# Eight decodings of a weight matrix moved to fixed units of the first batch and tied to the source's order

## The chip, the core and the metric

The kernel runs on one core of one Trainium2 chip. What counts is the device time of one execution in microseconds (us), as the median of several runs. The program is one straight line of instructions without loops at run time: TensorE (PE in the profile, its weight loads PEld), VectorE (DVE), ScalarE (ACT), GpSimd (POOL) and the queue that issues the transfers (SP) each take their own list of instructions in order, and wait for one another through semaphores.

## The reference

Causal block attention feeds a spatially gated block, which feeds a residual block of two dense layers. Batch 4, 8 heads, 576 positions, head dimension 64, all in float32:

```python
scores = scale * q @ k.T                      # masked by blocks of 64 positions
attn   = softmax(scores);  x = attn @ v       # heads joined: x is [4, 576, 512]
h      = relu(x @ w_in)                       # w_in [512, 1024]: u and v halves
gated  = u * (w_spatial @ normalize(v) + b_spatial)
x2     = gated @ w_out
out    = x2 + relu(normalize(x2) * g_ln @ w_ch1) @ w_ch2
```

## The kernel before, in words

**Decoding.** The weights arrive in device memory as 64-bit floats, that is, as pairs of 32-bit words. `decode` (line 81) makes a float32 out of such a pair: one ScalarE instruction on the high words (line 88), one VectorE shift on the low words (line 89), and one VectorE instruction that joins the two (line 90). `split` (line 94) then makes of every float32 a high part and a rest, which TensorE multiplies separately. For `w_in` both halves of the split are on GpSimd: a `tensor_scalar` (line 101) and a subtraction (line 102), since `PLAN['dh']` is `'g'`.

**The stage around the change.** `w_in` is decoded in eight pieces of 128x512 by the generator `decode_in` (line 420). Its first step only issues three loads of 512 KB from the SP queue (line 427); three buffers hold raw pieces (`bufs=3`, line 426). Each later step decodes and splits one piece and then issues the load three pieces ahead, so that the load of piece 3 waits until piece 0 has been read. The loop at line 532 runs over the units `u` of the attention: 16 pairs of heads (four batches of four), nine units to a pair. Unit 0 of a pair is the tail of 64 rows of both heads, the other eight are the four blocks of 128 rows of each head, the longest first. Each unit traces, in this order: the scores on TensorE (lines 250 to 281), the masked maximum on VectorE (line 296) and the exponential on ScalarE (line 303), the transposes of the unit two before it (line 353) with their copies out on VectorE (line 345, tails and blocks of index 3) or ScalarE (line 347, blocks of index 0 to 2), at unit 7 and unit 2 of a pair the product with v (line 404), at unit 5 the scaling and splitting of the pair before (`store_x`, lines 411 to 418, all on GpSimd: lines 414, 60 and 417), one step of `prepare` for the next pair (line 198: its `q` and `k` split, on VectorE line 56, ScalarE lines 58, 212 and 225, and GpSimd lines 209 or 221 and 223), and last the decoding, in the first four pairs at the units whose index in their pair leaves 1 when divided by 3 (`PLAN['pace']` is 3). So the loads start in unit 1, and the eight decodings are traced in units 4, 7, 10, 13, 16, 19, 22 and 25. The first products that need `w_in` are traced from unit 44 on (`value_tile`, line 445, matmuls of lines 106 to 108); they need all of `xT`, too, which `store_x` writes.

**The order on the engines.** The source gives each instruction its rank only. A planner in the build simulates the machine with its own estimates of durations and arrivals, and gives each engine (and the SP queue) its list: of what is ready by its estimate, the lowest rank goes first. An instruction can thus stand well before or behind its place in the source. The chip keeps to the list as it is. `tc.keep_in_program_order(ins)` ties one instruction behind the one traced just before it on its engine; what is traced later may still pass it. The other two users of `decode` (lines 640 and 700) give it that function as `here`; `decode_in` doesn't, and `here` is then a function that does nothing.

Of the kernel before, what the change touches and what calls it, by code (L numbers as in the profile page):

```python
# [19 lines left out]

PLAN = {'mm': 3, 'sc': 3, 'tr': 2, 'D': 2, 'hi0': 'v', 'hi1': 's', 'klo0': 'g', 'klo1': 'g', 'qlo0': 'g', 'qlo1': 'g', 'xm0': 'g', 'xm1': 'g', 'xh0': 'g', 'xh1': 'g', 'xl0': 'g', 'xl1': 'g', 'dm': 'g', 'dh': 'g', 'ev0': 3, 'ev1': 2, 'rate': 24500.0, 'vrb': 3, 'ds': 2, 'dy': 1, 'raw': 5, 'yn': 2, 'ts': 3, 'ring': 8, 'wt': 2, 'cb': 1, 'hq': 8, 'packed': 4, 'plain': 3, 'pre': 8, 'py': 10, 'pyn': 4, 'dn0': 2, 'dnn': 5, 'vl': 'v', 'pace': 3, 'wd': 7, 'tl0': 'v', 'tl1': 'v', 'xe': 's', 'pt': 6, 'dstart': 8}


def f32(ap):
    return ap.bitcast(F32)
# [8 lines left out]
def tile_kernel(  # L34
# [26 lines left out]
    NB, NP, _, _, _, S = qk.shape  # L61
# [19 lines left out]
    def decode(raw, m, e, out, here=lambda ins: ins):  # L81

        low, high = raw[:, :, 0], raw[:, :, 1]
        here(nc.scalar.activation(m, f32(high), AF.Prelu, scale=2.0**-112, alpha=2.0**32))  # L88
        here(nc.vector.tensor_scalar(e, low, 29, None, op0=ALU.logical_shift_right))
        nc.vector.scalar_tensor_tensor(  # L90
            out.bitcast(U32), m.bitcast(U32), 3, e, op0=ALU.logical_shift_left, op1=ALU.bitwise_or
        )

    def split(src, hi, lo, high="s", low="g"):

        if high == "s":
            nc.scalar.copy(hi, src)  # L97
        elif high == "v":
            nc.vector.tensor_copy(hi, src)
        else:  # L100
            nc.gpsimd.tensor_scalar(hi, src, 1.0, 0.0, op0=ALU.mult, op1=ALU.add)
        {"v": nc.vector, "g": nc.gpsimd}[low].tensor_tensor(lo, src, f32(hi), op=ALU.subtract)  # L102
# [80 lines left out]
    def warm(n):  # L183
        for _ in range(n):
            tc.keep_in_program_order(MM(idle, lhsT=zeros[:, 0:128], rhs=zeros, start=True, stop=True))
# [101 lines left out]
    def softmax(u):  # L287

        j, c = UNITS[u % NU]
        banks = state[u]  # L290
        sm = sums[u // NU]
        pt = tail if c == 4 else at.tile([128, 512], F32, tag="p", name="p", bufs=PLAN['pt'])
        nm = at.tile([128, 2], F32, tag="nm", name="nm", bufs=4)
        for i, (s_ps, o, n) in enumerate(banks):
            m = mask[:, 0:n] if c == 4 else mask[:, 512 - n:512]
            nc.vector.tensor_tensor_reduce(  # L296
                pt[:, o:o + n], s_ps[:, :n], m, -0.125, 3e38, ALU.add, ALU.min, nm[:, i:i + 1]
            )
        if c == 4:
            nc.vector.tensor_tensor(nm[:, 0:1], nm[:, 0:1], nm[:, 1:2], op=ALU.min)  # L300
        n = o + n
        col = 8 if c == 4 else 4 * j + c
        nc.scalar.activation(  # L303
            pt[:, :n], pt[:, :n], AF.Exp, bias=nm[:, 0:1], scale=-1.0, accum_out=sm[:, col:col + 1]
        )
        state[u] = (pt, n)
# [3 lines left out]
    def reciprocals(p):  # L310

        sm = sums.pop(p)
        nc.vector.tensor_scalar(sm, sm, 1e-9, None, op0=ALU.add)
        nc.vector.reciprocal(sm, sm)
        ps = p_tr.tile([128, 512], F32, tag="tr", name="rps")
        nc.tensor.transpose(ps[:9, :128], sm, idn)
        rr = at.tile([128, 128], F32, tag="rr", name="rr", bufs=1)
        nc.scalar.copy(rr[:9], ps[:9, :128])
        nc.sync.dma_start(out=r_d[p, :, 0:512].rearrange("j (c q) -> j c q", q=128), in_=rr[:8])
        nc.sync.dma_start(out=r_d[p, :, 512:S], in_=rr[8:9])  # L320
        rb = at.tile([128, S], F32, tag="rb", name="rb")
        for j in range(2):
            nc.sync.dma_start(out=rb[64 * j:64 * j + 64], in_=r_d[p, j].partition_broadcast(64))
        rb_t[p] = rb
# [13 lines left out]
    def transposes(u):  # L338
        j, c = UNITS[u % NU]
        pt, n = state.pop(u)  # L340

        def put(src, dst):
            out = dst(pT_of(u // NU)[1 if c >= 2 else 0])
            if c >= PLAN["ev1" if u >= NU * NP else "ev0"] and not (c == 4 and PLAN["tl1" if u >= NU * NP else "tl0"] == "s"):
                nc.vector.tensor_copy(out, src)  # L345
            else:
                nc.scalar.copy(out, src)

        def flip(k0, k1):
            tr = p_tr.tile([128, 512], F32, tag="tr", name="tr")  # L350
            for kc in range(k0, k1):
                o = 128 * (kc - k0)
                nc.tensor.transpose(tr[:, o:o + 128], pt[:, 128 * kc:128 * kc + 128], idn)  # L353
            return tr

        if c == 4:
            tr = flip(0, 4)
            put(
                tr.rearrange("p (r h q) -> p r h q", h=2, q=64),
                lambda t: view(t, 256, [[WH, 4], [5 * WH, 2], [1, 64]]),  # L360
            )
            tr = flip(4, 5)
            put(tr[:, 0:128].rearrange("p (h q) -> p h q", q=64), lambda t: t[:, :, 4 * WH + 256:5 * WH])
        else:
            tr = flip(0, c + 1)
            put(
                tr[:, :n].rearrange("p (r q) -> p r q", q=128),
                lambda t: view(
                    t, (5 * WH if c >= 2 else 2 * WL) * j + 128 * (c % 2), [[WH if c >= 2 else WL, c + 1], [1, 128]]
                ),  # L370
            )
# [5 lines left out]
    def tick():  # L377
        for e in list(slow):
            e[0] -= 1
            if e[0] <= 0:  # L380
                slow.remove(e)
                e[1]()

    def flush():
        todo, later[:] = list(later), []
        for f in todo:
            f()
# [32 lines left out]
    def decode_in():  # L420
        raws = {}

        def fetch(i):
            if i < 2 * KD:
                kc, h = divmod(i, 2)
                raws[i] = dn.tile([128, F, 2], U32, tag="hl", name="raw", bufs=3)
                nc.sync.dma_start(
                    out=raws[i].rearrange("p a b -> p (a b)"), in_=wi32[:, kc, 2 * F * h:2 * F * h + 2 * F]
                )

        fetch(0)
        fetch(1)
        fetch(2)
        yield
        for i in range(2 * KD):
            kc, h = divmod(i, 2)
            m = dn.tile([128, F], F32, tag="vr", name="dm", bufs=PLAN["vrb"])
            e = dn.tile([128, F], U32, tag="ur", name="de")
            cols = slice(F * h, F * h + F)
            decode(raws.pop(i), m, e, m)  # L440
            split(m, win[0][:, kc, cols], win[1][:, kc, cols], PLAN['dh'])
            fetch(i + 3)
            yield
# [57 lines left out]
    dense = None  # L501
    debt = 0.0
    dec = decode_in()
    preps = {}

# [23 lines left out]
    size = [200 + (S if c == 4 else 128 * (c + 1)) for _, c in UNITS]  # L529
    tot = float(sum(size) * NP)  # L530
    D = PLAN['D']
    for u in range(NS + 8):
        p, i = divmod(u, NU)
        if u < NS:
            scores(u)
            if u < 3:
                warm(3)
            softmax(u)
        tick()
        flush()  # L540
        if D <= u < NS + D:
            transposes(u - D)
        if i == PLAN['wd'] and p < NPAIR:
            weighted(p, 1)
        if i == 0 and 1 <= p <= NPAIR:
            reciprocals(p - 1)
        if i == D and 1 <= p <= NPAIR:
            weighted(p - 1, 0)
        if i == D + 3 and 1 <= p <= NPAIR:
            store_x(p - 1)  # L550
        if i == 0:
            for q in range(2, PACKED) if p == 0 else range(max(p + 2, PACKED), p + 3):
                load(q)
            load_v(p + 2)
            if p + 1 < NPAIR:
                preps[0] = prepare(p + 1)
        if 0 in preps and i >= 1:
            next(preps[0], None)
        if p < NP:
            if i % PLAN['pace'] == 1:  # L560
                next(dec, None)
        else:
            b, k = divmod(u, NU * NP)
            if k == PLAN['dstart'] and b <= NB - 1:
                dense = chain(dense, w_in_stage(b - 1))
            fill(PLAN['rate'] * size[i] / tot)
# [81 lines left out]
    dec = decode_out()  # L648
# [24 lines left out]
    raws = {}  # L673
# [441 lines left out]
def _layout(np, q, k, v, moe_w_in, moe_w_spatial, moe_b_spatial, moe_w_out, moe2_g_ln, moe2_w_ch1, moe2_w_ch2):  # L1115

    B, H, S, D = q.shape
    qk = np.stack([q, k], axis=2).reshape(B, H // 2, 2, 2, S, D).transpose(0, 1, 5, 2, 3, 4)
# [40 lines left out]
```

## Time and profile before

| what | value |
|---|---|
| device time, median of 3 runs | 808.03 us (807.02 to 809.18) |
| the profiled execution's own time | 806.9 us |
| its span in the profile | 805.0 us |
| TensorE busy | 783.6 us (97%) |
| VectorE, ScalarE, GpSimd busy | 526.8, 420.3, 414.6 us |

The span runs from the first to the last instruction of the profiled execution; its own time has 1.9 us more around it. Times in rows are microseconds from the start of the span unless a column says ns. An engine's share of the whole span is a mean over stages with different limits; for this change the first 85 us are what to look at. The granted clock (PEclk) is TensorE's, as a share of full speed, with 1.00 for 2.4 GHz and 0.50 for 1.2 GHz.

### The profile page before, as it was taken

What the parts mean: (1) busy time and instruction counts of PE and PEld (TensorE: products, weight loads), DVE (VectorE), ACT (ScalarE), POOL (GpSimd) and SP (SyncE); (2) the same over time, 40 slices, a digit from 0 to 9 for tenths busy, and PEclk for the clock granted to TensorE, in tenths of its full rate; (3) what the DMA queues carried; (4) which work ended last, traced back from release to release, by engine and by line L of the source; (5) the groups of instructions that cost most, each with busy time, mean ns of one, the idle gap of its engine ahead of it and who ended that gap; (6) DMA issues with size and microseconds to landing.
All of it is one profiled execution on the core that took longest, in us unless ns stands there. A gap on an engine that the chain in (4) does not pass through costs nothing.

```text
span 805.0 us, 13277 instructions
## 1 busy us (share of the span) xinstructions
PE 783.6 (97%) x4498; PEld 671.3 (83%) x4498; DVE 526.8 (65%) x1193; ACT 420.3 (52%) x1071; POOL 414.6 (51%) x417
## 2 busy tenths in 40 slices
PE   9899999999999999899999999999999999999997
PEld 4567788778878799899988888888899888888986
DVE  5866666674565277776677787897566588645534
ACT  5688676566755454555363554553344454433421
POOL 5799656654553343232275455455545465545431
PEclk9799999999999999999999999999999999999999
DMA  8927645445241569688520343204001003000002
GB/s 236 257 66 191 177 126 159 127 140 160 67 157 61 151 210 291 208 250 271 173 92 1 97 125 94 79 0 157 1 15 39 1 1 127 18 0 1 1 1 78
DMA packets 53687, 88.66 MB, mean 110 GB/s; under 512 B 6770, under 2 KB 17138, under 8 KB 53620
## 3 DMA queue, kind: packets, MB, share of 16 engines
q1 hardware_dynamic: 53620, 87.83, 36.7%
q8 instruction: 35, 0.57, 0.3%
q14 instruction: 32, 0.26, 0.1%
HBM read 68.85 MB, written 18.95 MB: 109 GB/s over the span
## 4 chain that ended last, share of the span: by engine, by line
PE 76%; DMA 7%; DVE 7%; issue 3%; POOL 3%; SPq 2%; ACT 2%; POOLq 0%; ACTq 0%; DVEq 0%
PE hps L938 21%; PE o L106 8%; PE o L108 8%; PE o L107 8%; PE pv L404 5%; PE tr L353 4%; PE sc L281 3%; DMA raw<-in_w_in_dram 2%; PE ups L106 2%; PE by L106 2%; PE ups L108 2%; PE ups L107 2%; PE by L108 2%; PE by L107 2%; DMA raw<-in_w_ch_dram 1%
## 5 line engine op out<-in xcount | busy, mean ns | idle before, releaser
L102 POOL TENSOR_TENSOR a<-s,a 128x256 fp32r<-128x256 f32 x96 | 78.2, 818 | 93.3 <-ACT a L97 93.3
L107 PE MATMUL o<-w,h 128*128 128x512 f32 x288 | 112.9, 393 | 0.0
L106 PE MATMUL o<-w,h 128*128 128x512 f32 x288 | 107.8, 398 | 1.4 <-ACT h L930 1.4
L944 DVE TENSOR_TENSOR c<-hps,c 128x384 f32<-128x384 f32 x120 | 66.5, 554 | 55.0 <-PE hps L938 53.3
L108 PE MATMUL o<-w,h 128*128 128x512 f32 x288 | 97.6, 397 | 0.2
L296 DVE CUSTOM_DVE_ANT_0 p<-sc,mask 128x512 f32<-128x512 f32 (+3 forms) x128 | 58.6, 478 | 43.2 <-PE sc L281 21.0
L303 ACT ACTIVATE p<-p,nm 128x512 f32<-128x512 f32 (+3 forms) x128 | 71.2, 558 | 28.4 <-DVE nm L296 25.8
L102 POOL TENSOR_TENSOR a<-w,a 128x256 fp32r<-128x256 f32 x72 | 60.7, 845 | 44.7 <-ACT a L97 38.7
L97 ACT CAST a<-s 128x256 fp32r<-128x256 f32 x96 | 38.4, 404 | 83.5 <-PE hps L938 75.3
L345 DVE COPY pH<-tr 128x512 f32<-128x512 f32 (+1 forms) x88 | 49.8, 574 | 24.7 <-PE tr L353 23.9
L106 PEld LDWEIGHTS o<-w,h 128*128 128x128 f32 x288 | 53.7, 188 | 12.0 <-ACT h L930 2.7
L107 PEld LDWEIGHTS o<-w,h 128*128 128x128 f32 x288 | 54.1, 188 | 10.1
L353 PE MATMUL tr<-idn,p 128*128 128x128 f32 x320 | 56.4, 283 | 6.1 <-DVE pH L345 6.1
L108 PEld LDWEIGHTS o<-w,h 128*128 128x128 f32 x288 | 53.2, 188 | 8.8 <-DVE h L931 1.0
L788 POOL TENSOR_TENSOR gt<-gf,gt 128x576 fp32r<-128x576 f32 (+1 forms) x17 | 25.3, 1493 | 60.7 <-ACT gt L787 60.7
L117 POOL TENSOR_TENSOR rs<-rs,nhalf 128x1 f32<-128x1 f32 x36 | 23.5, 654 | 62.6 <-DVE rs L116 62.4
L353 PEld LDWEIGHTS tr<-idn,p 128*128 128x128 f32 x320 | 38.4, 142 | 16.6 <-DVE pH L345 8.5
L88 ACT ACTIVATE dm<-raw 128x256 f32<-128x256 f32 (+1 forms) x72 | 32.1, 464 | 32.4 <-DVE w L90 8.8
L221 POOL TENSOR_TENSOR stack<-qkt,stack 64x576 fp32r<-64x576 f32 x24 | 34.0, 1417 | 26.1 <-ACT stack L58 23.7
L931 DVE SCALAR_TENSOR_TENSOR h<-c,h 128x384 fp32r<-128x384 f32 x72 | 44.7, 642 | 1.5 <-ACT h L930 1.5
L281 PE MATMUL sc<-stack 128*128 128x512 f32 (+3 forms) x192 | 43.8, 342 | 0.8 <-DVE nm L296 0.2
L930 ACT ACTIVATE h<-c 128x384 fp32r<-128x384 f32 x72 | 35.3, 521 | 16.2 <-DVE c L944 15.9
(183 smaller groups left out, 2265.8 us busy)
## 6 DMA issues: line engine op xcount, KB each, us to landing
raw<-in_w_ch_dram SPq DMA_DIRECT2D x64, 256.0 KB
qkt<-in_qk_dram SPq DMA_DIRECT2D x112, 144.0 KB
vt<-in_v_dram SPq DMA_DIRECT2D x16, 320.0 KB
rb<-r_d SPq DMA_DIRECT2D x32, 144.0 KB
u_d<-ur SPq DMA_DIRECT2D x16, 288.0 KB
us<-u_d SPq DMA_DIRECT2D x16, 288.0 KB
y_d<-ys SPq DMA_DIRECT2D x18, 256.0 KB
yr<-y_d SPq DMA_DIRECT2D x18, 256.0 KB
```

The costliest lines, as they stand in the source:

```text
L102: {"v": nc.vector, "g": nc.gpsimd}[low].tensor_tensor(lo, src, f32(hi), op=ALU.subtract)
L106: MM(out_ps, lhsT=a[0], rhs=b[0], start=first, stop=False)
L107: MM(out_ps, lhsT=a[0], rhs=b[1], start=False, stop=False)
L108: MM(out_ps, lhsT=a[1], rhs=b[0], start=False, stop=last)
L281: MM(s_ps[:, :nn], lhsT=st[:, j, i, q], rhs=st[:, j, 2, 0:nn], start=(i == 0), stop=(i == 1))
L296: nc.vector.tensor_tensor_reduce(pt[:, o:o + n], s_ps[:, :n], m, -0.125, 3e38, ALU.add, ALU.min, nm[:, i:i + 1])
L303: nc.scalar.activation(pt[:, :n], pt[:, :n], AF.Exp, bias=nm[:, 0:1], scale=-1.0, accum_out=sm[:, col:col + 1])
L345: nc.vector.tensor_copy(out, src)
L353: nc.tensor.transpose(tr[:, o:o + 128], pt[:, 128 * kc:128 * kc + 128], idn)
L931: nc.vector.scalar_tensor_tensor(t[:, 1], src, 0.0, f32(t[:, 0]), op0=ALU.max, op1=ALU.subtract)
L938: MM(ps, lhsT=a[x], rhs=b[y], start=not more and kc == 0 and k == 0, stop=kc == KD // 2 - 1 and k == 2, skip_group_check=True,)
L944: nc.vector.tensor_tensor(out, ps, x, op=ALU.add)
```

## The change

`decode_in` now passes `tc.keep_in_program_order` to `decode`, so that the ScalarE instruction and the VectorE shift of each piece are tied behind what was traced just before them on their engine. And the decodings no longer follow the rhythm of three: the loads still start in unit 1, and the eight decodings are traced in units 8, 12, 16, 20, 23, 26, 29 and 32.

```diff
@@ decode_in @@
-            decode(raws.pop(i), m, e, m)
+            decode(raws.pop(i), m, e, m, tc.keep_in_program_order)
@@ before the loop over the units @@
+    DECODE = {1, 8, 12, 16, 20, 23, 26, 29, 32}
@@ in the loop, after the step of prepare @@
-        if p < NP:
-            if i % PLAN['pace'] == 1:
-                next(dec, None)
-        else:
+        if u in DECODE:
+            next(dec, None)
+        if p >= NP:
             b, k = divmod(u, NU * NP)
```

## Rows read from the trace of the kernel before

**Rows 1.** The page: span, busy time of each engine.

```profile
span 805.0 us, 13277 instructions
...
PE 783.6 (97%) x4498; PEld 671.3 (83%) x4498; DVE 526.8 (65%) x1193; ACT 420.3 (52%) x1071; POOL 414.6 (51%) x417
```

**Rows 2.** The chain that ended last, 12 to 60 us: start, length, what.

```profile
15.06 8.81 DMA raw<-in_w_in_dram
...
24.47 8.08 DMA raw<-in_w_in_dram
```

**Rows 3.** Stretches between three products with v: length, busy (count) by engine, clock, DMA.

```profile
20.27:38.35 18.08, 14.86 (x79) 9.74 (x78) 14.52 (x35) 11.02 (x33) 14.03 (x14) 0.77 1.04 259
38.35:52.48 14.13, 13.79 (x91) 9.27 (x90) 11.18 (x35) 12.15 (x33) 12.32 (x12) 0.93 0.50 121
52.48:64.37 11.89, 11.54 (x84) 8.42 (x83) 7.97 (x30) 10.29 (x31) 11.31 (x11) 1.00 0.26 77
```

**Rows 4.** The same view in steps of 2 us: PE, PEld, DVE, ACT, POOL, clock.

```profile
24.00:26.00 2.00, 1.47 (x14) 1.13 (x13) 2.00 (x6) 2.00 (x7) 2.00 (x3) 1.00 1.02 274
26.00:28.00 2.00, 1.62 (x9) 1.08 (x9) 2.00 (x3) 0.70 (x4) 2.00 (x2) 0.65 1.09 204
28.00:30.00 2.00, 2.00 (x11) 1.29 (x11) 1.01 (x4) 0.74 (x2) 2.00 (x3) 0.50 1.01 220
30.00:32.00 2.00, 0.91 (x6) 0.47 (x5) 2.00 (x4) 0.88 (x4) 2.00 (x2) 1.00 1.02 248
32.00:34.00 2.00, 0.77 (x5) 0.54 (x6) 1.44 (x6) 0.97 (x2) 1.71 (x2) 0.86 1.02 364
34.00:36.00 2.00, 2.00 (x9) 1.78 (x9) 2.00 (x9) 1.37 (x5) 0.55 (x3) 0.50 1.00 338
36.00:38.00 2.00, 2.00 (x6) 1.09 (x5) 0.94 (x5) 1.05 (x2) 2.00 (x4) 0.50 1.05 245
38.00:40.00 2.00, 2.00 (x8) 0.80 (x9) 2.00 (x4) 1.54 (x4) 1.23 (x1) 0.50 1.04 225
```

**Rows 5.** Waits, 20 to 43 us: engine line <- releaser: us, times, longest.

```profile
ACT dm L88 <- DMA raw<-in_w_in_dram: 4.7, 3, 2.6
...
DVE de L89 <- DMA raw<-in_w_in_dram: 2.4, 3, 1.0
```

**Rows 6.** ScalarE in order of time: start, length, line, out<-in.

```profile
20.20 0.70 ACT L88 ACTIVATE dm<-raw 128x512 f32<-128x512 f32 x1
...
24.78 0.57 ACT L347 COPY pL<-tr 128x256 f32<-128x256 f32 x2
...
40.22 0.78 ACT L303 ACTIVATE tail<-tail,nm 128x576 f32<-128x576 f32 x1
...
42.23 0.66 ACT L88 ACTIVATE dm<-raw 128x512 f32<-128x512 f32 x1
```

**Rows 7.** The decodings' instructions, 0 to 60 us: ns min/median/max, first and last start.

```profile
L89 DVE TENSOR_SCALAR de<-raw x8: 361/528/1055, 19.9 to 40.2; 128x512 uint32<-128x512 uint32 x8
...
L88 ACT ACTIVATE dm<-raw x8: 663/676/700, 20.2 to 42.2; 128x512 f32<-128x512 f32 x8
L90 DVE SCALAR_TENSOR_TENSOR dm<-dm,de x8: 679/817/1293, 21.8 to 44.4; 128x512 uint32<-128x512 uint32 x8
L101 POOL TENSOR_SCALAR win<-dm x8: 618/784/1119, 22.6 to 46.6; 128x512 fp32r<-128x512 f32 x8
L102 POOL TENSOR_TENSOR win<-dm,win x8: 1261/1366/1733, 24.1 to 49.0; 128x512 fp32r<-128x512 f32 x8
```

**Rows 8.** GpSimd in order of time: start, length, line, idle before and releaser.

```profile
22.58 1.59 POOL L101 TENSOR_SCALAR win<-dm 128x512 fp32r<-128x512 f32 x2 [3.55 <-DVE dm L90]
...
65.30 1.41 POOL L223 TENSOR_TENSOR stack<-qkt,stack 64x576 fp32r<-64x576 f32 x1
...
80.48 1.42 POOL L417 TENSOR_TENSOR xT<-xx,xT 128x576 fp32r<-128x576 f32 x1
```

**Rows 9.** TensorE in order of time.

```profile
68.92 0.71 PE L260 MATMUL sc<-stack,qtail 128*128 128x256 f32 x4
...
81.51 0.41 PE L106 MATMUL vps<-win,xT 128*128 128x512 f32 x1
```

## The prediction, made before the changed kernel ran

> **What bounds the kernel now.** Read the page first: TensorE is busy for 783.6 of 805.0 us [rows 1]. Over the whole span it is the bound, so the change can only win where TensorE stands idle or runs slowly, 21.4 us of idleness in all and whatever the clock takes. The chain of waits says where to look: between 15.06 and 32.55 us it consists almost wholly of two transfers of w_in's raw pieces, 8.81 and 8.08 us long [rows 2]. The only things that wait for these pieces are the decodings on ScalarE (4.7 us in three waits) and on VectorE (2.4 us in three) [rows 5]. Both engines take their lists in order, so the exponentials, the maxima and the copies of transposes that stand behind a decoding wait with it, and TensorE waits for those.
>
> The stretch table prices this. From one pair's first product with v to the next takes 18.08, 14.13 and 11.89 us [rows 3]; only the first two hold decodings (the last one's copy on ScalarE is at 42.23 [rows 6]). Against the third the two are 8.43 us longer together. In steps of 2 us the same loss shows as idleness and as clock [rows 4]. TensorE is idle for 0.53, 0.38, 1.09 and 1.23 us in the steps from 24, 26, 30 and 32, in all 3.2. The granted clock falls to its lower level of 1.2 GHz after those gaps and is back at 2.4 GHz only after 40 us; busy time times what the clock lacks is 0.57 + 1.00 + 0.11 + 3 x 1.00 = 4.7. Together 7.9 us, close to 8.4. That is all that the change can win at this place.
>
> **Why the waits are there.** By rank the eighth decoding belongs to unit 25. On ScalarE it is at 42.23, right after unit 18's exponential (the tail one at 40.22) [rows 6]. The planner let the later decodings run ahead of their rank because by its estimate their data had come; on the chip they had not, with the transfer engines busy throughout (the next-to-last column of rows 4 is 1.00 or above).
>
> **The change part by part.** No instruction is added or removed: eight times one ScalarE copy (0.68 us), two VectorE instructions (0.53 + 0.82 = 1.35 us by the medians, 1.04 to 2.35 by the ends) and two on GpSimd (0.78 + 1.37 = 2.15 us) [rows 7] move, and with them five of the eight loads on the SP queue, each of which follows the decoding three pieces before it.
>
> The units. Decodings 5 to 8 are tied to units 23, 26, 29 and 32, six to twelve units later than they run now. A piece is loaded nine to twelve units before its decoding. At 11.89 us for nine units [rows 3] this is 11.9 us or more, against the 8.1 to 8.8 us that a piece takes [rows 2]. So the DMA waits of the fourth to the eighth decoding should go, and the second and third have had their pieces since 23.87 us. The first is tied behind the copy of unit 6's transpose, which is at 24.78, where now it runs at 20.20 [rows 6]; its piece has come by then, too. What a later load pushes on the SP queue (the loads of q and k, the reciprocals' way through memory) I cost at nothing: the queue now holds these behind the same loads, which issue into full transfer engines.
>
> What is late next. With TensorE's gaps closed, the three stretches of rows 3, 44.10 us, have to hold the same work of the other engines: GpSimd 14.03 + 12.32 + 11.31 = 37.7, VectorE 33.7, ScalarE 33.5, TensorE at full clock 40.2 - 4.7 = 35.5. GpSimd has the most. Of its 6.4 us of idleness, 2.3 lie ahead of the first decoding's split (from 20.27 to 22.58 [rows 8]) and stay, so it could end at most 4.1 earlier. TensorE may gain a little more than GpSimd: pair 5's last split on GpSimd ends at 65.30 + 1.41 = 66.7 and TensorE uses it at 68.92 [rows 8, 9], a slack of 2.2. The bounds are therefore 2.2 (none of the idleness filled) and 6.3 us (all of it). I take the middle, 2.2 + 2.1 = 4.3, since the spread decodings fill some of the holes and leave others.
>
> Against that stands ScalarE in the stretch that now has no decoding. It is busy for 10.29 of 11.89 us there [rows 3] and gets two copies, 1.35 us, which leaves 0.25. In a list with waits that may lengthen the stretch by 0 to 1.35; I take half, 0.7. VectorE goes from 7.97 to 10.7 of 11.89 and is covered; if the cover fails, its price is inside the same bounds. Sum: 4.3 - 0.7 = 3.6 us gained, with bounds 0.9 (2.2 - 1.35) and 6.3. After the first batch TensorE is busy nearly without a break, and what it gains early it keeps.
>
> One rule speaks against the change. The VectorE shift has taken from 0.36 to 1.05 us and the join from 0.68 to 1.29, on the same shape [rows 7], and GpSimd is busy in 11.31 of 11.89 us where two decodings now go, against 14.03 of 18.08 where they ran [rows 3]. The Trainium skill (SBUF — State Buffer, "Who interferes with whom") says that VectorE in its two-port modes, or with two SBUF inputs against a GpSimd instruction that reads SBUF, shares one port pair with GpSimd, and that whoever starts first blocks the other. The spread of the row agrees; by the rule, estimated from the row's upper ends, the two moved decodings would take 2 x 1.0 us more on VectorE and the gain would be 1.6 us instead of 3.6.
>
> **The predicted time.** The profiled execution took 806.9 us and so would take 803.3. The median of the runs shown, 808.03, is 1.1 above it; on that scale I predict 804.4. Below, 0.3% of 808.03 is 2.4 us, about what a measurement of this kernel can tell from no change: faster means below 805.6, slower above 810.5.
>
> **The rivals.** *A, GpSimd takes back most.* It is busy all along the third stretch, 11.31 of 11.89 us, and two decodings' splits, 4.3 us, move in. If its holes before are not filled, the gain is between the lower bound and the threshold, 0.9 to 2.4 us: 805.6 to 807.1. For it speaks that GpSimd is the fullest engine; against it, that TensorE has a slack of 2.2 us. Chance 0.18.
>
> *B, the waits stay, or the tie does not hold the decodings.* The tie reaches only to the one instruction traced before, which may itself run early, and a later load may land later. Then one wait of some microseconds takes the place of another: 808, give or take 1.5. Against it: most ties here are to the same unit's maximum or to a copy two units back, which cannot run before their scores. Chance 0.15.
>
> *C, GpSimd starts late and TensorE ends up waiting for it; this one is slower.* If the first decoding slips from 20.20 to behind 24.78 [rows 6], GpSimd's idleness before its split grows by up to 4.6 us. GpSimd then runs nearly without a break until store_x of pair 3 ends at 80.48 + 1.42 = 81.9 [rows 8], and the value products of that pair begin at 81.51 [rows 9]: no slack is left there. What GpSimd loses early, TensorE would wait for at that place, 4.6 us at most and 2.4 if the 2.2 of slack could be used: 810.4 to 812.6, and 811.5 in the middle. It decides if GpSimd finds no other work (the next pair's splits, store_x of pair 0) in that hole. For it: its chain from 43 to 82 us is unbroken. Against it: that other work exists, and TensorE would only lose if nothing else stood in its list. Chance 0.17.
>
> **How the numbers follow.** The forecast, a gain of 2.4 to 6.3 us, has a chance of 0.5 and a range of its own of 801.7 to 805.6. A and B give no difference that can be measured, 0.18 + 0.15 = 0.33. C gives slower, 0.17. The range has to reach over A and B and to C's lower end: 801.0 to 810.5, which takes 0.7 below the forecast's own bound because the planner makes the whole order anew from unit 8 on, and leaves out most of C.
>
> **What would show it.** Right: in the changed profile no wait of lines 88 and 89 for the raw pieces after 24 us; the clock at 1.00 from 20 to 50 us; the second and third product with v less than 14 us after the one before; the fourth by 3 to 6 us earlier than 64.37; GpSimd without long idleness between 22 and 60 us. Wrong: waits of line 353 for line 345 with the clock down to 0.50 again; a wait of TensorE for GpSimd at the first scores of pairs 4 and 5, or ahead of the first value products; or the early gain there and gone by the end of the first value tiles. A decoding that stands more than two units off its unit would say that the tie does not hold.

## The result: slower, and where the time went

The changed kernel takes 818.61 us (816.99 to 820.4, 4 runs) against 807.67 us (807.02 to 809.18) of the kernel before, a ratio of 1.0136 [1.0111, 1.0161]. The prediction said 804.4 with a range of 801.0 to 810.5: it was wrong in sign and outside the range. The profiled execution took 818.46 us, with this page:

```profile
span 816.6 us, 13279 instructions
...
PE 786.9 (96%) x4498; PEld 673.5 (82%) x4498; DVE 535.8 (66%) x1193; ACT 420.6 (52%) x1071; POOL 414.0 (51%) x417
```

Against [rows 1] TensorE's busy time has grown by 3.3 us only, so most of the 11.6 us of longer span is idleness of TensorE. VectorE, with the same 1193 instructions, is busy for 9.0 us more; ScalarE and GpSimd are where they were, to within 0.6 us. The stretches between products with v (columns as in [rows 3]: length, then busy time and count of PE, PEld, DVE, ACT, POOL, then the granted clock, the DMA share and GB/s) show the place:

```profile
19.73:33.80 14.07, 12.88 (x83) 8.53 (x82) 9.05 (x28) 9.65 (x31) 6.02 (x7) 0.88 0.85 209
33.80:53.90 20.10, 15.59 (x90) 10.17 (x88) 17.10 (x37) 11.52 (x32) 16.90 (x17) 0.80 0.74 182
53.90:74.04 20.14, 15.88 (x84) 11.27 (x84) 14.54 (x33) 12.53 (x34) 15.10 (x14) 0.70 0.32 86
74.04:86.11 12.07, 10.57 (x80) 7.96 (x79) 8.45 (x29) 9.42 (x28) 10.09 (x9) 1.00 0.43 118
```

The first stretch fell from 18.08 us [rows 3] to 14.07, a gain of 4.0. The second rose from 14.13 to 20.10 and the third from 11.89 to 20.14. Over these two, TensorE's idleness (length less busy time) went from 0.34 + 0.35 = 0.7 us to 4.51 + 4.26 = 8.8, and the part of its busy time that the clock lacks (busy time by 1 less the granted clock) from about 1.0 to 15.59 x 0.20 + 15.88 x 0.30 = 7.9. Together that is 15.0 us, where the stretches are 14.2 longer. So somewhat over half is idleness, and the rest is the clock. From the fifth product with v to the end the two kernels take the same, 729.7 us before and 730.5 after.

In steps of 2 us (same columns) one sees idleness and clock side by side:

```profile
36.00:38.00 2.00, 1.28 (x13) 0.79 (x9) 2.00 (x3) 1.05 (x4) 2.00 (x2) 1.00 1.03 183
38.00:40.00 2.00, 0.62 (x3) 0.41 (x3) 1.68 (x8) 1.53 (x4) 1.92 (x3) 1.00 1.02 246
...
42.00:44.00 2.00, 2.00 (x12) 1.67 (x12) 0.92 (x4) 2.00 (x6) 1.05 (x1) 0.57 0.24 55
44.00:46.00 2.00, 2.00 (x13) 1.31 (x10) 2.00 (x4) 1.54 (x3) 1.73 (x2) 0.58 0.01 1
46.00:48.00 2.00, 0.50 (x5) 0.26 (x3) 2.00 (x2) 0.00 (x0) 1.29 (x2) 1.00 0.74 153
48.00:50.00 2.00, 1.57 (x9) 1.28 (x9) 2.00 (x9) 1.32 (x4) 1.93 (x2) 0.78 0.90 310
50.00:52.00 2.00, 2.00 (x6) 1.12 (x5) 2.00 (x5) 0.85 (x4) 1.92 (x2) 0.50 0.68 182
...
62.00:64.00 2.00, 1.22 (x8) 0.69 (x7) 0.95 (x3) 1.78 (x5) 1.97 (x3) 0.69 0.29 74
64.00:66.00 2.00, 2.00 (x12) 1.36 (x9) 2.00 (x3) 0.37 (x1) 2.00 (x2) 0.50 0.43 148
66.00:68.00 2.00, 1.08 (x6) 0.68 (x4) 2.00 (x2) 0.00 (x0) 1.93 (x2) 0.50 0.58 164
68.00:70.00 2.00, 0.47 (x2) 0.47 (x3) 2.00 (x5) 0.20 (x1) 1.92 (x3) 0.50 0.00 0
70.00:72.00 2.00, 2.00 (x11) 1.96 (x10) 1.30 (x8) 1.73 (x6) 1.92 (x2) 0.50 0.00 0
```

Two holes of one kind stand out, at 46 to 50 and at 66 to 70. In both VectorE is busy without a break, at first with only two instructions in 2 us, and ScalarE does nothing in 46 to 48 and 66 to 68. They hold 1.9 and 2.5 us, half of the 8.8 us of idleness. The other half lies at 36 to 42 (2.6 us) and at 58 to 64 (1.8 us). The clock is low in 42 to 46, behind the hole at 36 to 42; in 50 to 56, behind the first of the two; and from 62 to 73, which begins before the second of the two, behind the idleness at 58 to 64. The instructions in order of time, around the first of the two holes and then around the second (start, length, engine, line; in brackets the idle time before and what ended it):

```profile
43.80 0.29 DVE L345 COPY pH<-tr 128x128 f32<-128x128 f32 x1 [0.16 <-PE tr L353]
44.01 1.96 DVE L89 TENSOR_SCALAR de<-raw 128x512 uint32<-128x512 uint32 x2
44.20 1.48 POOL L221 TENSOR_TENSOR stack<-qkt,stack 64x576 fp32r<-64x576 f32 x1 [0.90 <-ACT stack L58]
45.75 1.47 POOL L223 TENSOR_TENSOR stack<-qkt,stack 64x576 fp32r<-64x576 f32 x1
45.89 1.89 DVE L90 SCALAR_TENSOR_TENSOR dm<-dm,de 128x512 uint32<-128x512 uint32 x1
47.70 0.68 DVE L345 COPY pH<-tr 128x512 f32<-128x512 f32 x1
48.43 0.55 PE L353 MATMUL tr<-idn,p 128*128 128x128 f32 x3 [1.94 <-DVE pH L345]
48.67 0.40 ACT L303 ACTIVATE p<-p,nm 128x128 f32<-128x128 f32 x1 [3.02 <-DVE nm L296]
...
63.84 1.40 POOL L417 TENSOR_TENSOR xT<-xx,xT 128x576 fp32r<-128x576 f32 x1
63.95 3.12 DVE L89 TENSOR_SCALAR de<-raw 128x512 uint32<-128x512 uint32 x2
65.20 1.58 POOL L221 TENSOR_TENSOR stack<-qkt,stack 64x576 fp32r<-64x576 f32 x1
66.86 1.47 POOL L223 TENSOR_TENSOR stack<-qkt,stack 64x576 fp32r<-64x576 f32 x1
66.99 1.89 DVE L90 SCALAR_TENSOR_TENSOR dm<-dm,de 128x512 uint32<-128x512 uint32 x1
68.80 0.68 DVE L345 COPY pH<-tr 128x512 f32<-128x512 f32 x1
69.53 0.69 PE L353 MATMUL tr<-idn,p 128*128 128x128 f32 x2 [2.45 <-DVE pH L345]
69.80 0.40 ACT L303 ACTIVATE p<-p,nm 128x128 f32<-128x128 f32 x1 [4.19 <-DVE nm L296]
```

Both are the same picture. Behind the small copy of a tail's transpose (line 345, 128x128) VectorE has two shifts and one join in a row, and only then the next block's copy. TensorE's transposes (line 353) wait for that copy, 1.94 and 2.45 us, and ScalarE's exponential for the maximum behind it, 3.02 and 4.19 us. Three decoding instructions that need 2 x 0.37 + 0.69 = 1.4 us undisturbed (minima of the next rows, 0.366 and 0.685) hold the list for 3.7 us (44.01 to 47.70) and 4.9 us (63.95 to 68.80). They are long beside GpSimd: the join that starts at 45.89, just behind the start of a GpSimd subtraction (45.75), ends 0.6 us after that subtraction; the one at 66.99 does the same (66.86 + 1.47 = 68.33, and 68.88). The decodings' own rows (ns min/median/max, first and last start) cover all eight:

```profile
L89 DVE TENSOR_SCALAR de<-raw x8: 366/614/1628, 19.3 to 65.4; 128x512 uint32<-128x512 uint32 x8
L88 ACT ACTIVATE dm<-raw x8: 652/668/696, 22.7 to 70.8; 128x512 f32<-128x512 f32 x8
L90 DVE SCALAR_TENSOR_TENSOR dm<-dm,de x8: 685/1469/1889, 24.8 to 72.0; 128x512 uint32<-128x512 uint32 x8
L101 POOL TENSOR_SCALAR win<-dm x8: 608/618/939, 25.6 to 75.2; 128x512 fp32r<-128x512 f32 x8
L102 POOL TENSOR_TENSOR win<-dm,win x8: 1267/1279/1652, 26.3 to 77.7; 128x512 fp32r<-128x512 f32 x8
```

Against [rows 7] the join's median rose from 0.82 to 1.47 us and the shift's maximum from 1.06 to 1.63, while ScalarE's and GpSimd's instructions did not grow. The waits of lines 88 and 89 for the raw pieces, 7.1 us in [rows 5], are gone altogether.

The hole at 36 to 42 has no lump, that is, no row of several decoding instructions. A single join, started just behind a GpSimd split (line 102, 35.94 to 37.22), is long in the same way and ends 0.55 us after that split. TensorE waits for the maximum behind the join:

```profile
36.03 1.74 DVE L90 SCALAR_TENSOR_TENSOR dm<-dm,de 128x512 uint32<-128x512 uint32 x1
...
38.43 0.62 PE L275 MATMUL sc<-stack 64*128 64x256 f32 x3 [1.15 <-DVE nm L296]
```

Between 58 and 64 TensorE and VectorE wait for one another in steps below 0.8 us; what makes that stretch so thin stays open.

Why the instructions stand in a lump can be read in the source. The tie holds a shift behind what was traced just before it on VectorE. In a unit of index 2 (units 20 and 29) that is not the unit's own maximum but the copy of the tail's transpose, two units back in the source, which VectorE reaches late. So the shifts of units 20 and 29 stand there. That the shifts of units 23 and 32, whose tie is to their own maximum, stand right behind them is seen in the trace and not worked out; with units 20 and 29 moved (e7 below) all stand singly.

### The profile page after: what moved, and what is told of

Its sections match the earlier page's. It is cut to its first block, busy times and chain, and to the rows that moved or that the text cites. A ratio compares the mean times of both kernels' runs of the same rounds, so it can differ in the third digit from the quotient of the medians.

```text
span 816.6 us, 13279 instructions
## 1 busy us (share of the span) xinstructions
PE 786.9 (96%) x4498; PEld 673.5 (82%) x4498; DVE 535.8 (66%) x1193; ACT 420.6 (52%) x1071; POOL 414.0 (51%) x417
## 4 chain that ended last, share of the span: by engine, by line
PE 75%; DVE 8%; DMA 7%; issue 3%; POOL 3%; SPq 2%; ACT 2%; POOLq 0%; DVEq 0%; ACTq 0%
PE hps L938 21%; PE o L106 8%; PE o L108 8%; PE o L107 7%; PE pv L404 4%; PE tr L353 4%; PE sc L281 3%; DMA qkt<-in_qk_dram 2%; PE by L106 2%; PE by L107 2%; PE by L108 2%; PE sps L108 2%; PE sps L106 2%; PE sps L107 2%; PE ups L106 2%
```

## The experiments

Two theories were set against each other. **H**: the tie puts the decodings as a lump at the hand-over between a tail and the next blocks, where TensorE and ScalarE wait for VectorE. **G**: at the late units GpSimd is busy most of the time (16.90 of 20.10 us), so that every shift and join takes longer wherever it stands. All ratios are to the kernel before on the same chip, which took 806.5 to 807.8 us; they can differ by up to 0.2% from the quotient of the two medians.

**Each half of the change alone.** First the tie with the old units, then the new units without the tie.

```diff
# e1_tie_only: the tie, decodings at units 4, 7, ... 25
+            decode(raws.pop(i), m, e, m, tc.keep_in_program_order)
# e2_units_only: the new units, no tie
+    DECODE = {1, 8, 12, 16, 20, 23, 26, 29, 32}
```

> The tie alone, with the decodings at their old units. Theory H (hand-over): what costs is that decodings, two shifts and a join in a row, stand on VectorE between the copies of a tail's transposes and the copy of the next block, where TensorE waits for a free bank. Here every decoding stands alone on VectorE, so H expects 803 to 808 us. Theory G (GpSimd beside it): what costs is that VectorE's shifts and joins run late, from 44 us on, where GpSimd is always busy, and each waits for a GpSimd instruction to end. Here the last join runs at about 50 us instead of 72, so G expects 808 to 812.

> The new units alone, without the tie. VectorE's list is then nearly that of the kernel before, since the planner places a decoding by its estimate of the arrival. H and G both expect the time before, 806 to 809 us, and the waits of lines 88 and 89 for the raw pieces back. If the later units by themselves cost anything, 811 or more.

e1 took 805.08 us, 0.998 [0.9956, 1.0005]; e2 810.93, 1.004 [1.0018, 1.0062], 2 us above what was expected. e1 is where H put it, and below G. In e1 the waits for the raw pieces fell from 7.1 to 2.7 us. In e2, where the planner was free, most of them came back:

```profile
ACT dm L88 <- DMA raw<-in_w_in_dram: 4.7, 2, 3.8
...
DVE de L89 <- DMA raw<-in_w_in_dram: 1.8, 1, 1.8
```

So neither half makes the loss: one gives -0.2%, the other +0.4%, and both together +1.36%.

**The tie on one engine.**

```diff
+    def tie_one(ins):     # e5: Activation only; e6: all but Activation
+        return tc.keep_in_program_order(ins) if ins.ins.engine == mybir.EngineType.Activation else ins
-            decode(raws.pop(i), m, e, m, tc.keep_in_program_order)
+            decode(raws.pop(i), m, e, m, tie_one)
```

> The change with the tie on ScalarE alone. VectorE's shifts then stand singly and none of the decodings' instructions stands between a tail's copies and the next block's, while the joins run as late as in the change. H (lumps at the hand-over) expects 804 to 810 us, G (late work beside a busy GpSimd) 812 to 819.

> The change with the tie on VectorE alone. At the tails of pairs 2 and 3 a shift and a join still stand between the tail's copies and the next block's, two instructions instead of three. H expects most of the loss to stay, 812 to 818 us; G 812 to 819 as well.

ScalarE's tie alone gives 811.42, 1.0036 [1.0017, 1.0054], no different from e2, and between the two theories' numbers; VectorE's alone 816.77, 1.010 [1.0067, 1.0133], as both said. Most of the loss beyond the units' comes from VectorE's tie.

**Same units, no lump.** e3 traces the decoding right behind the unit's masked maximum, so that the tie is to that. e7 only moves two of the units away from index 2.

```diff
# e3_tie_to_max: ahead of the transposes, instead of at the unit's end
+        if u in DECODE:
+            next(dec, None)
# e7_off_tail
-    DECODE = {1, 8, 12, 16, 20, 23, 26, 29, 32}
+    DECODE = {1, 8, 12, 16, 19, 23, 26, 28, 32}
```

> New units and tie as in the change, but the decoding is traced right behind its unit's exponential, ahead of the transposes, so that the VectorE tie is to the unit's own maximum and no longer to the copies of a tail. The decodings are then spread singly over VectorE's list, as late as in the change. H expects the early gain kept and the later loss gone: 801 to 805 us. G expects the loss to stay, since the last ones run beside a busy GpSimd as before: 812 to 819.

> The changed kernel with two of its units moved by one, 20 to 19 and 29 to 28, so that no shift is tied behind a tail's copies; both lumps dissolve, and the last joins run as late as before. H expects 804 to 811 us, G 814 to 819 since nothing runs earlier by more than a unit.

e3 took 810.32 us, 1.0023 [0.9991, 1.0055], between the two theories' numbers; e7 811.37, 1.0024 [1.0005, 1.0044], just above what H said and below G's. The runs of e3 spread widely, from 801.6 to 815.2 us. Taking the lump away gives back 1.1 of the 1.4%, in e7 by moving two units only: H has the larger share, but not all. The four kernels with the new units and without the two lumps (e2, e3, e5, e7) lie at 1.0023 to 1.004.

**Same lump, a freer GpSimd.** The subtractions of lines 221 and 223 are left out for pairs 4 and 5, so the low parts of these pairs stay uncomputed: eight instructions fewer on GpSimd, once with the lump (e4), once without it (e10), and as a control in the kernel before (e15).

```diff
+            if p >= PACKED + 2:
                 nc.gpsimd.tensor_tensor(st[low, j, 0, :], raw[low, j, 0, :], ...)
...
+            if p >= PACKED + 2:
                 nc.gpsimd.tensor_tensor(st[high, j, 2, :], raw[high, j, 1, :], ...)
```

> The changed kernel without the four GpSimd subtractions (lines 221 and 223) for each of pairs 4 and 5, so that the low parts of their q and k are not computed; VectorE's list keeps its lumps, GpSimd has 11 us less between 42 and 85 us. G expects the joins and shifts back at 0.4 and 0.7 us and the time at 804 to 808. H expects only the part of the wait that the lumps have by their own length to stay, 1.5 us at each of three places with the clock's fall behind it: 810 to 814.

> The spread decodings at the new units (the tie to the unit's own maximum) without the eight GpSimd subtractions for pairs 4 and 5, so that the low parts of their q and k are not computed. What is left of the loss when the lumps are gone is 2 to 4 us. G says that this rest comes from shifts and joins that wait for GpSimd: 801 to 806 us. If the rest is in the order itself, in the clock or in late data, 808 to 812.

> The kernel before without the subtractions of the low parts (L221 and L223) for pairs 4 and 5, so their low parts are left uncomputed. If GpSimd's subtractions cost time only beside the late decodings, this is 805 to 808 us, no different from before; if it is a general relief (every product chain of the first 75 us freed), it gains what e4 and e10 gained, some 8 us: 797 to 801 us. Between 801 and 805 us part of either.

| | with the lump | without it | old units, no tie |
|---|---|---|---|
| all subtractions | 1.0136 [1.0111, 1.0161] (the change) | 1.0023 [0.9991, 1.0055] (e3) | 1 (before) |
| eight left out | 1.0027 [1.0002, 1.0053] (e4) | 0.9936 [0.9907, 0.9965] (e10) | 1.0003 [0.998, 1.0027] (e15) |

e4 took 808.46 us, between the two theories' numbers; e10 took 802.26, as G said; e15 took 807.13, no different from before. Down a column, the subtractions cost 1.1% and 0.9% in the kernels with late decodings and nothing in the kernel before, where they run after the decodings are over (the last join starts at 44.4, [rows 7]). Along a row, the lump costs 1.1% and 0.9%, though e3 and e10 move the ties of all eight decodings and not of the two lumps alone.

At the lumps e4 shows how lump and subtractions belong together (start and length as before; line 347 here is line 345 elsewhere, 355 is 353):

```profile
43.88 0.77 DVE L89 TENSOR_SCALAR de<-raw 128x512 uint32<-128x512 uint32 x2
44.55 0.70 DVE L90 SCALAR_TENSOR_TENSOR dm<-dm,de 128x512 uint32<-128x512 uint32 x1
45.16 0.70 DVE L347 COPY pH<-tr 128x512 f32<-128x512 f32 x1
...
45.91 0.55 PE L355 MATMUL tr<-idn,p 128*128 128x128 f32 x3 [0.57 <-DVE pH L347]
```

The lump is still there, but it lasts 1.3 us (43.88 to 45.16) instead of 3.7, and TensorE waits 0.57 us behind it instead of 1.94; the second one lasts 1.3 us (58.55 to 59.84) instead of 4.9. In e7, with the subtractions and without the lumps, TensorE's longest wait for line 345 between 20 and 80 us is 0.9 us. So the two long holes needed both: the lump, and the subtractions beside it.

For what is left without the lump, G's way is not shown. Here are the rows of shifts and joins, of e4 and then of e10:

```profile
L89 DVE TENSOR_SCALAR de<-raw x8: 364/433/1918, 20.0 to 58.9; 128x512 uint32<-128x512 uint32 x8
L90 DVE SCALAR_TENSOR_TENSOR dm<-dm,de x8: 686/1138/1934, 25.5 to 64.5; 128x512 uint32<-128x512 uint32 x8
```

```profile
L89 DVE TENSOR_SCALAR de<-raw x8: 421/1023/2177, 19.1 to 55.3; 128x512 uint32<-128x512 uint32 x8
L90 DVE SCALAR_TENSOR_TENSOR dm<-dm,de x8: 681/688/1029, 21.0 to 57.9; 128x512 uint32<-128x512 uint32 x8
```

In e10 the median join is back at 0.69 us, but the shifts are longer than in the change (1.02 us against 0.61), and in e4 the joins away from the lumps stay long. Shifts and joins together take 15.8 us in e3 and 15.1 in e10, 0.7 us less for a gain of 7. Nor does that sum go with the time in the other kernels: e5 and e7 have 12.0 and 12.9 us, near the 11.7 of the kernel before, and are slower than it; e9 (below) has 15.3 and is not. In e3 the loss stands in one stretch:

```profile
50.16:68.10 17.94, 15.40 (x82) 11.00 (x81) 11.95 (x29) 11.04 (x32) 17.36 (x18) 0.71 0.34 102
```

TensorE is idle for 2.5 us there, and the clock takes 15.40 x 0.29 = 4.5. That the eight subtractions cost some 0.9% there is measured; by which path is open.

**The lump at the old units.** e9 is e1 with the decoding behind the maximum; e11 is e1 with two units moved so that the tie falls behind a tail's copy.

```diff
# e9_old_units_max: as e3, with
+    DECODE = {1, 4, 7, 10, 13, 16, 19, 22, 25}
# e11_early_lump: as e1, with
+    DECODE = {1, 4, 7, 11, 13, 16, 20, 22, 25}
```

> The old units with the tie to the unit's own maximum and exponential: no lumps, and the last join some ten units earlier than in the change. H expects what the runs with dissolved lumps have or less, 801 to 807 us; G expects the gain of the earlier place on top, 801 to 805, and clearly below the runs with late units.

> The tie with the old units, but with 10 moved to 11 and 19 to 20, so that a shift is tied behind the copies of a tail, and a shift and a join stand between those and the next block's at the tails of pairs 1 and 2; nothing else runs later than with the old units. H expects 808 to 813 us, clearly over the tie with the old units. G expects no difference from that, 803 to 808.

e9 took 806.07, 0.9969 [0.994, 0.9997]; e11 808.68, 1.0026 [1.0, 1.0053], as H said and just above G. Two units moved by one make 0.5 to 0.6%, about 4 us (the intervals of e11 and e9 do not overlap, those of e11 and e1 just do), and the trace of e11 (in order of time) shows the hand-over again, with TensorE behind it:

```profile
42.86 0.29 DVE L345 COPY pH<-tr 128x128 f32<-128x128 f32 x1 [0.45 <-PE tr L353]
43.06 1.40 DVE L89 TENSOR_SCALAR de<-raw 128x512 uint32<-128x512 uint32 x1
44.57 0.69 DVE L90 SCALAR_TENSOR_TENSOR dm<-dm,de 128x512 uint32<-128x512 uint32 x1
45.18 0.68 DVE L345 COPY pH<-tr 128x512 f32<-128x512 f32 x1
46.01 0.52 PE L353 MATMUL tr<-idn,p 128*128 128x128 f32 x3 [1.37 <-DVE pH L345]
```

**Is lateness itself the fault?** e14 is e9 with only the last two decodings late.

```diff
# e14_last_two_late: as e9, with
+    DECODE = {1, 4, 7, 10, 13, 16, 19, 29, 32}
```

> The old units with the tie to the unit's own maximum, but the last two decodings at units 29 and 32 as in the change. G expects the rest of the loss from these two, which run beside a busy GpSimd: 808 to 812 us. If the rest comes from the middle decodings, tied to 20 to 26, then 803 to 808.

It took 805.86, 0.9971 [0.9947, 0.9996], the same as e9. Both late decodings' shifts and joins stand in the second of these two stretches, one earlier decoding's in the first; both stretches are as long as [rows 3]'s third, which has none (columns as there):

```profile
39.87:51.63 11.76, 11.41 (x85) 8.05 (x84) 9.04 (x32) 11.24 (x33) 10.75 (x11) 1.00 0.69 175
51.63:63.35 11.72, 11.37 (x85) 8.32 (x84) 10.04 (x30) 10.78 (x32) 11.36 (x12) 1.00 0.42 116
```

So a late decoding behind a maximum costs nothing at the end of the batch, where G put the rest of the loss. That what is left in e3 comes from the decodings at units 8 to 26 follows from this only by subtraction, and e3's interval overlaps e14's.

**Versions that might beat both.** e12 puts the decodings' first split on ScalarE (on top of e9), e16 the zero fills of line 217 on VectorE (on top of e14).

```diff
# e12_high_on_scalar
-'dh': 'g'
+'dh': 's'
# e16_zeros_on_vector
-            nc.gpsimd.memset(f32(st[high, :, 0, :]), 0.0)
+            nc.vector.memset(f32(st[high, :, 0, :]), 0.0)
```

> The old units with the tie to the unit's own maximum, and the high half of w_in's split on ScalarE instead of GpSimd, which takes eight instructions of 0.62 us off GpSimd. If GpSimd still limits the stretches between 20 and 65 us, 802 to 805 us; if ScalarE, full in the third stretch, takes its place, 806 to 810.

> e14 with the zero fills of L217 on VectorE instead of GpSimd. If GpSimd's list is what delays the moved decodings, less of it gives 802 to 805 us; if VectorE's own list is what counts, its longer list gives 806 to 810 us.

e12 took 810.59, 1.0041 [1.0017, 1.0064], 0.6 us above what was expected if ScalarE, with its 10.29 of 11.89 us [rows 3], has no room for it; that this is the reason was not tested by itself. e16 took 806.34, 0.9986 [0.996, 1.0012], no better than e14. The best with the whole computation are e9 and e14, 0.3% below the kernel before and 1.6% below the changed one (0.9971 / 1.0136 = 0.984).

## Why the prediction was wrong, step by step

- **"The DMA waits of the fourth to the eighth decoding should go": right.** None is left, and the first stretch gained 4.0 us. That this is close to the 4.3 of the sum is chance: the 4.3 was the middle between two bounds for all three stretches.
- **"VectorE goes from 7.97 to 10.7 of 11.89 and is covered; if the cover fails, its price is inside the same bounds": this is the step that failed.** It priced two decodings by the medians of [rows 7] and by a share of busy time. VectorE was busy for 17.10 and 14.54 us in the two stretches, 9.0 us more over the span, 5.9 of it in the shifts and joins (17.6 us in all against 11.7 before) and 4.5 in two small instructions (lines 300 and 313), while others took a little less. And a share of busy time says nothing of the place: 3.7 and 4.9 us at the one point where TensorE and ScalarE have nothing but VectorE to wait for are not covered by idleness elsewhere in the stretch. The runs put most of the loss there: without the lump 1.1 of the 1.4% are gone (e7, e3), and without the subtractions beside it as much (e4). The price, 14.2 us in two stretches, was far outside the bounds of 0 to 1.35.
- **"Most ties here are to the same unit's maximum or to a copy two units back, which cannot run before their scores": true, and read the wrong way.** It was used to show that the decodings would be late enough. That a tie to a copy makes them later still, with a second piece behind them in front of the next copy, was not asked; e3, e7 and e11 show that it matters. One reading beside it was off: by [rows 6] the eighth decoding moves from behind unit 18 to unit 32, fourteen units and not twelve at most. Nothing in the sum hung on it.
- **The weighed rule: the rule was right and its size too small.** The trace shows joins of 1.89 us that end 0.6 us after a GpSimd subtraction. The Trainium skill (SBUF — State Buffer, "Who interferes with whom") has VectorE and GpSimd share a port pair that whoever starts first holds; the rows of these joins agree. The prediction made 2 us of it and set it aside for the main sum, where 5.9 us came. e4 shows that the long lumps go when the subtractions beside them go. That the shared ports are the reason, and not something else that goes with a busy GpSimd, no run tests.
- **The clock.** The prediction took the clock's loss as part of the gain (4.7 us before). The same kind of loss came back, 7.9 us in the two stretches, each time behind idleness of TensorE, and not only behind the two lumps. That it follows the idleness is read from the trace and was not tested by itself.
- **The rivals.** C had the sign and the wrong mechanism. GpSimd did start late (its first split at 25.60 instead of 22.58 [rows 8]), but the place where C saw TensorE wait, the first value products, lies behind the fifth product with v, and from there on the two kernels take the same (729.7 and 730.5 us). B's condition (the tie does not hold) did not come about, and A's price (a gain between 0.9 and 2.4 us) did not either. No rival had VectorE as the bound, although "waits of line 353 for line 345 with the clock down to 0.50 again" stood among the signs that would show the forecast wrong, and is what came.

## What to carry to other kernels

Before an instruction is tied to "what was traced just before", write down for each place what that is, and what stands behind it on the same engine: a tie to something that itself runs late gathers work in front of whoever waits. Price a moved instruction by its longest row beside the engine that it now runs beside, not by its median elsewhere, and look at the place in the list as well as at the busy share. And test units and tie separately: here one was harmless, the other cheap, and only together were they dear.

## What the runs showed that was not expected

- A 128x512 join on VectorE that takes 0.69 us by itself takes up to 1.89 us beside GpSimd's 1.4 to 1.5 us subtractions; two shifts that need 0.7 took 3.12 us. A 128x9 instruction of VectorE (line 313) took 1.88 us beside a GpSimd multiplication.
- Eight GpSimd instructions of some 1.4 us left out give 0.9 to 1.1%, 7 to 9 us, in the kernels with late decodings, and 0.0% [-0.2, +0.3] in the kernel before. What they cost depends on what else runs at that time.
- TensorE's clock took 7.9 us in the two long stretches, nearly as much as the 8.8 us of idleness: it was granted at 0.50 for most of 50 to 56 and 63 to 72 us, and at 0.57 in 42 to 46, each time behind idleness of TensorE (at 36 to 42, 46 to 50 and 58 to 64).
